# A linear-attention and MLP kernel: k and q loaded as bf16 by casting DMAs and left unscaled, the decay moved to v and to the attention output, stores of 64 rows from SyncE

## The chip, the cores and the metric

The kernel runs on one core of a Trainium2 chip. The metric is the device time in microseconds (us). Before the change it was 261.36 us, the median of two runs (261.17 to 261.54). Profiles come from one execution each; their span is about 2 us shorter than the device time of the same run (259.0 for 260.8). All times below that carry a position ("at 73.4 us") are counted from the start of that span.

## The reference, cut to what matters

```python
# q, k, v: (B=4, H=8, S=768, D=64) float32; lam: (8,), about 0.97 to 0.99
for b in range(S // 64):                       # blocks of 64 positions
    intra = (q_b @ k_b^T) * lam**(i - j) [i >= j] @ v_b
    inter = (q_b * lam**(i + 1)) @ kv_state
    out_b = intra + inter
    kv_state = lam**64 * kv_state + (k_b * lam**(63 - i))^T @ v_b
x = out as (3072 tokens, 512)
h = x @ w_in                                   # 512 -> 2048
g = h + sin(alpha * h)**2 / (alpha + 1e-9)
return g @ w_out                               # 2048 -> 512, float32
```

## The kernel before

The kernel works on blocks of 128 positions and pairs of batches. One *step* is half the heads of one block: transposes of q and k ("T"), scores ("S"), then outputs and the state ("O"). Four steps fill one *chunk* of 512 tokens. A chunk's first matmul is 16 *A groups* (x times w1, four matmuls each), its second 16 *B groups* (g times w2). There are six chunks, 0 to 5; while TensorE works on chunk c, it also does the steps of chunk c+1. The steps 0 to 3 have nothing to hide behind, and steps 4 to 7 are done in the B part of chunk 0.

In the views, PS is a bank of PSUM (the memory that TensorE writes its results to), S_m are the masked scores, xT is the attention output as the first matmul reads it, Zacc the state and Zs its bf16 copy, u and t are steps of the sine and its square, gT is g, and osb is an output tile.

A small planner in Python records every operation with an assumed duration, sorts by planned start time, and emits a fixed order for each engine. Each engine then runs its list strictly in that order. So an assumed duration that is wrong costs nothing in itself, but it can put an instruction that has to wait ahead of one that is ready.

```python
        # decay: q scaled by lam**i, k by lam**-i, per position of the pass; v only cast
        def prep_x(s, x, engs=("POOL", "DVE")):          # x is "q" or "k"
            ...
            rec(eng, lambda e: e.tensor_tensor(dst[c][:, :, :], raw(src, s), L_b, ALU.mult), dur, ...)

        def load(d, x, parts=(0, 1), eng="SP", after=()):  # float32, 64 partitions per DMA
            ...
            nbytes=29375 * nh      # what the planner counts, nh = 8 heads: 235,000

        # attention output, a plain copy on ScalarE
        op = rec("ACT", lambda e: e.copy(xo, xi), 0.6, ...)

        # the store of one output tile
        dst = bass.AP(out.tensor, row0 * DM, [[DM, 2], [2 * DM, 64], [1, DM]])
        rec("ACT", lambda e: e.dma_start(dst, osb[o][:, :]), 0, ...)

        # start: loads of blocks 2 and 3 wait for the third w2 block
        for m0, n in ((0, 2), (2, 2), (4, 4), (8, 4), (12, 4)):
            w1_block(m0, n, after=[v0])
        for j in range(4):
            w2b = w2_block(4 * j, 4, after=[v0])
            if j == 2:
                gate = w2b
        for x in "kqv":
            for d in (2, 3):
                load(d, x, after=[gate])
```

An access pattern is a list of [step, count], slowest first. The store's destination has two as its slowest count: token rows 0, 2, 4, ... come from partitions 0 to 63 and rows 1, 3, 5, ... from partitions 64 to 127. The weights are loaded by GpSimd, which casts them to bf16 on the way.

## Time and profile before

The timeline gives the positions below. "First w1 matmul" is the first A group of chunk 0, and each chunk is counted from its first A group to that of the next chunk.

| stretch | before, us |
|---|---|
| start, to the first w1 matmul | 23.8 |
| chunk 0 | 49.6 |
| chunks 1 to 4 | 138.5 |
| chunk 5, to the end of the last matmul | 30.4 |
| tail, to the end of the span | 16.7 |

The lines below are from the page of the kernel before: busy time of each engine, then the span in 40 equal slices of 6.5 us (busy tenths of TensorE, the TensorE clock that was granted in tenths, and the mean busy share of the 16 DMA engines in tenths), then the DMA queues with their share of 16 engines' span.

```profile
PE 216.0 (83%) x2785; PEld 108.6 (42%) x2785; DVE 136.0 (53%) x190; ACT 129.2 (50%) x203; POOL 119.2 (46%) x137
PE   0448897299589999999999999999999999999400
PEclk9999999658959999999999999999999999999955
DMA  6999999999349996944355110001101011010111
q1 hardware_dynamic: 38016, 18.88, 34.1%
q0 software_dynamic: 4752, 4.19, 10.5%
q10 hardware_dynamic: 3296, 6.30, 6.6%
```

TensorE (PE) is the busiest engine, yet it is full only from the thirteenth slice on. From the second to the tenth slice the row of the DMA engines is full and the row of TensorE is not. At the end TensorE has nothing to do and the DMA row reads 1.

The next view is the table of busy time by stretch, with its header; the first line is the tail, the others ten-microsecond stretches of chunk 0.

```profile
core 0: us, PE busy (x) PEld busy (x) DVE busy (x) ACT busy (x) POOL busy (x), PEclk, DMA share, GB/s
242.40:259.00 16.60, 0.00 (x0) 0.00 (x0) 0.00 (x0) 0.55 (x1) 0.00 (x0) 0.57 0.12 48
...
40.00:50.00 10.00, 3.95 (x19) 1.57 (x16) 3.78 (x6) 0.00 (x0) 4.82 (x5) 0.84 1.06 212
50.00:60.00 10.00, 9.57 (x126) 4.71 (x128) 3.32 (x5) 3.32 (x5) 4.50 (x5) 0.50 1.21 233
60.00:70.00 10.00, 7.89 (x217) 4.58 (x216) 5.97 (x9) 2.34 (x4) 1.83 (x3) 0.98 0.62 156
```

In the tail a share of 0.12 is two engines of sixteen. From 40 to 60 us the share is 1.06 and then 1.21, so the DMA engines are taken to be full (it adds up the times of the packets, and passes 1 where they overlap). TensorE waits from 44 to 50 us, and from 50 to 60 it runs at half its clock.

Finally the chain that ended last, in order of time (start, duration, what). It shows what chunk 0 hung on.

```profile
21.44 17.99 DMA w<-in_moe_w_out_dram
...
56.26 13.87 DMA v<-in_v_dram
70.18 0.62 POOL v L388
70.80 0.36 POOL Zs L549
71.20 0.64 PE PS L428 x8
```

The first line is the wait for w2, behind which the loads of blocks 2 and 3 are held.

### The profile page before, as it was taken

How to read it: one execution, taken by the hardware profiler on the slowest of the kernel's cores; microseconds unless marked ns; L12 is line 12 of the kernel's file. 1: busy time of each engine (PE TensorE's matmuls, PEld its weight loads, DVE VectorE, ACT ScalarE, POOL GpSimd, SP SyncE). 2: the span in 40 equal slices, each digit the busy share in tenths (PEclk: the TensorE clock that was granted, in tenths of full speed). 3: DMA queues.
4: the chain of work that ended last, by engine and by line, in shares of the span. 5: the costliest groups of instructions: out<-in, count | busy, mean ns of one | idle time of the engine just before them, and what ended most of it. 6: DMA issues, size and time to landing. Idle time of an engine off the chain costs nothing.

```text
span 259.0 us, 6365 instructions
## 1 busy us (share of the span) xinstructions
PE 216.0 (83%) x2785; PEld 108.6 (42%) x2785; DVE 136.0 (53%) x190; ACT 129.2 (50%) x203; POOL 119.2 (46%) x137
## 2 busy tenths in 40 slices
PE   0448897299589999999999999999999999999400
PEld 0346343145244445544455544555445544444100
DVE  2582595227317866557754677843687315850000
ACT  5045781040237764377826678446774447642000
POOL 3567764543246784446565464532744107440000
PEclk9999999658959999999999999999999999999955
DMA  6999999999349996944355110001101011010111
GB/s 138 226 166 172 206 206 188 227 228 220 99 154 194 224 193 186 229 134 143 97 157 150 53 51 21 34 12 49 51 17 42 3 43 51 31 40 18 51 51 44
DMA packets 46092, 29.79 MB, mean 115 GB/s; under 512 B 1504, under 2 KB 42992, under 8 KB 46064
## 3 DMA queue, kind: packets, MB, share of 16 engines
q1 hardware_dynamic: 38016, 18.88, 34.1%
q0 software_dynamic: 4752, 4.19, 10.5%
q10 hardware_dynamic: 3296, 6.30, 6.6%
q8 instruction: 22, 0.36, 0.6%
q14 instruction: 6, 0.05, 0.1%
HBM read 27.28 MB, written 6.29 MB: 130 GB/s over the span
## 4 chain that ended last, share of the span: by engine, by line
PE 65%; DMA 15%; SPq 9%; POOL 2%; ACT 1%; issue 1%
PE PS L614 28%; PE PS L577 28%; SPq L298 9%; DMA v<-in_v_dram 8%; DMA w<-in_moe_w_out_dram 7%; PE PS L406 3%; PE PS L438 2%; PE PS L415 2%; POOL w L359 2%; PE PS L428 2%; PE PS L451 1%; POOL w L364 1%; ACT qkT L560 0%; POOL v L388 0%; ACT xT L540 0%
## 5 line engine op out<-in xcount | busy, mean ns | idle before, releaser
L614 PE MATMUL PS<-w,gT 128*128 128x512 bf16 x384 | 93.2, 387 | 0.0
L589 POOL TENSOR_TENSOR u<-t 128x512 bf16<-128x512 bf16 x66 | 67.5, 1041 | 49.8 <-ACT t L581 48.6
L577 PE MATMUL PS<-xT,w 128*128 128x512 bf16 x384 | 88.5, 385 | 2.2 <-ACT xT L540 1.4
L591 DVE SCALAR_TENSOR_TENSOR gT<-u,r_sb,PS 128x512 bf16<-128x512 bf16 x96 | 69.1, 745 | 34.9 <-POOL u L589 34.4
L581 ACT ACTIVATE t<-PS,alpha_sb 128x512 bf16<-128x512 f32 x96 | 63.8, 683 | 23.7 <-PE PS L577 23.0
L577 PEld LDWEIGHTS PS<-xT,w 128*128 128x128 bf16 x384 | 37.7, 99 | 49.3 <-issue 3.8
L614 PEld LDWEIGHTS PS<-w,gT 128*128 128x128 bf16 x384 | 35.9, 99 | 42.6 <-issue 1.8
L523 DVE TENSOR_TENSOR S_m<-PS,mask 128x1024 bf16<-128x1024 f32 x24 | 29.3, 1224 | 29.0 <-PE PS L415 28.8
L540 ACT CAST xT<-PS 128x512 bf16<-128x512 f32 x24 | 14.1, 586 | 39.3 <-PE PS L438 39.2
L406 PE MATMUL PS<-ident,q 64*64 64x64 bf16 x384 | 15.4, 212 | 17.8 <-DVE q L381 17.2
L381 POOL TENSOR_TENSOR k<-k,Lk 128x512 bf16<-128x512 f32 x16 | 17.7, 1107 | 27.4 <-DMA k<-in_k_dram 13.0
L560 ACT COPY qkT<-PS 128x1024 bf16<-128x1024 bf16 x17 | 17.3, 1016 | 16.9 <-PE PS L406 15.8
L406 PEld LDWEIGHTS PS<-ident,q 64*64 64x64 bf16 x384 | 10.4, 119 | 29.0 <-POOL k L381 9.6
L621 ACT COPY osb<-PS 128x512 f32<-128x512 f32 x24 | 14.2, 591 | 16.2 <-PE PS L614 13.6
L428 PE MATMUL PS<-S_m,v 64*64 64x128 bf16 x384 | 14.6, 239 | 3.2 <-POOL Zs L549 3.2
L381 DVE TENSOR_TENSOR q<-q,Lq 128x512 bf16<-128x512 f32 x16 | 11.5, 741 | 10.0 <-DMA q<-in_q_dram 10.0
L438 PE MATMUL PS<-qkT,Zs 64*64 64x128 bf16 x160 | 15.6, 234 | 0.4
L549 POOL CAST Zs<-Zacc 128x256 bf16<-128x256 f32 x16 | 8.0, 498 | 16.5 <-DVE Zacc L547 16.5
L406 PE MATMUL PS<-ident,k 64*64 64x64 bf16 x384 | 14.6, 207 | 0.0
L415 PE MATMUL PS<-qkT 64*64 64x128 bf16 x384 | 13.5, 238 | 1.1 <-ACT qkT L560 0.4
L451 PE MATMUL PS<-v,k 64*64 64x64 bf16 x320 | 11.5, 207 | 1.7 <-issue 1.7
L428 PEld LDWEIGHTS PS<-S_m,v 64*64 64x64 bf16 x384 | 10.5, 118 | 5.8 <-POOL Zs L549 3.7
(40 smaller groups left out, 119.7 us busy)
## 6 DMA issues: line engine op xcount, KB each, us to landing
k<-in_k_dram SPq DMA_DIRECT2D x24, 256.0 KB, 6.5
q<-in_q_dram SPq DMA_DIRECT2D x24, 256.0 KB, 7.1
v<-in_v_dram SPq DMA_DIRECT2D x24, 256.0 KB, 7.1
out_dram<-osb ACTq DMA_DIRECT2D x24, 256.0 KB
w<-in_moe_w_out_dram POOLq DMA_DIRECT2D x4, 512.0 KB, 17.1
w<-in_moe_w_in_dram POOLq DMA_DIRECT2D x3, 512.0 KB, 9.7
w<-in_moe_w_in_dram POOLq DMA_DIRECT2D x2, 256.0 KB, 5.0
lam_bc<-in_lam_dram ACTq DMA_DIRECT2D x1, 4.0 KB, 2.8
```

Of the source, the lines that this page charges most:

```text
L298: op = rec(eng, lambda e, u=u, a=a: e.dma_start(dst[r][half(u), h0:h0 + nh, :], a), 0, writes=[f"{x}32.{r}.{u}.{p}" for p in parts], slot= ...
L381: rec(eng, lambda e: e.tensor_tensor(dst[c][:, :, :], raw(src, s), L_b, ALU.mult), dur, reads=reads, writes=writes)
L406: last = e.transpose(dst, src[half(u), hid(h, tt), :], ident[half(u), half(u)])
L415: return e.matmul(PS[half(u), sb_ + r, (h // 2 * 2 + tj) * 128:(h // 2 * 2 + tj + 1) * 128], qt[half(r), u, 1, h // 2, half(tj)], qt[half( ...
L428: return e.matmul(dst, v2[o % RC][half(u), hid(h, tj), :], S_m[o % RS][half(u), h % 2 ^ u, h // 2, tj, :], start=start, stop=True, skip_gr ...
L438: return e.matmul(dst, Zs[(o - 2) % 3][half(r), u, h // 2, :], qkT[o % RQ][half(r), u, 0, h // 2, :], start=start, stop=True, skip_group_c ...
L523: rec("DVE", lambda e: e.tensor_tensor(S_m[s % RS][:, :, :, :, :].rearrange("p r a t i -> p (r a) (t i)"), PS[:, sb_:sb_ + 2, :].rearrange ...
L577: last = e.matmul(PS[:, i, :], w1[:, kc, 128 * m:128 * (m + 1)], xT[x][:, kc, :], start=(kc == 0), stop=(kc == NKC - 1))
L581: rec("ACT", lambda e: e.activation(t16[tt][:, :], PS[:, i, :], ACTF.Sin, scale=alpha_sb[:, m:m + 1]), 0.7, reads=bk(i) + ["alpha"], write ...
L589: return e.tensor_tensor(u16[tt][:, :], t16[tt][:, :], t16[tt][:, :], ALU.mult)
L591: rec("DVE", lambda e: e.scalar_tensor_tensor(out=gT[g][:, m, :], in0=u16[tt][:, :], scalar=r_sb[:, m:m + 1], in1=PS[:, i, :], op0=ALU.mul ...
L614: last = e.matmul(PS[:, bank, :], gT[g][:, m, 128 * s4:128 * (s4 + 1)], w2[:, m, :], start=(m == 0), stop=(m == NM - 1))
```

## The change

The intent is to take work off the engines in the crowded first 75 us, and to order the loads better. In detail:

- k and q are loaded by GpSimd DMAs that cast to bf16, and are not scaled. The decay is put on v (lam**-j, one multiplication per step) and on the attention output (lam**i, as the output is moved out of PSUM, now on VectorE). A table of lam**i is built at the start.
- Loads of k and q and the weights of chunk 0 are issued one after another on GpSimd, interleaved; squares of chunk 0's A part leave GpSimd for ScalarE and VectorE.
- Each store becomes two of 64 rows, from SyncE.
- The planner counts a float32 load of half a block as 310,000 units instead of 235,000, and a cast load as 171,000. It also keeps the DMA issues of an engine in the order in which they were recorded, and lets a read of a PSUM bank wait for earlier reads of it by other engines.

```diff
-        q2 = ring("q2", RC, [128, 2 * HS, D], BF16)
+        q2 = ring("q2", RL, [128, H, 2 * D], BF16)
...
-                         nbytes=29375 * nh, after=after)
+                op = rec("SP" if x == "v" else "POOL", lambda e, u=u, a=a: e.dma_start(dst[r][half(u), :, :], a), 0,
+                         writes=[f"{x}.{r}.{u}"], slot=f"{x}{r}", nbytes=310000 if x == "v" else 171000, after=after)
...
-        def prep_x(s, x, engs=("POOL", "DVE")):
+        def prep_v(s, engs=("POOL", "DVE")):
+            rec(eng, lambda e: e.tensor_tensor(v2[c][:, :, :], src, L_b, ALU.mult), dur, reads=reads, writes=writes)
...
-                op = rec("ACT", lambda e: e.copy(xo, xi), 0.6, reads=keys_o,
+                rec("DVE", lambda e: e.tensor_tensor(xo, xi, X_b, ALU.mult), 0.72,
...
-                dst = bass.AP(out.tensor, row0 * DM, [[DM, 2], [2 * DM, 64], [1, DM]])
-                rec("ACT", lambda e: e.dma_start(dst, osb[o][:, :]), 0,
+                for t in range(2):
+                    dst = bass.AP(out.tensor, (row0 + t) * DM, [[2 * DM, 64], [1, DM]])
+                    rec("SP", lambda e, t=t, dst=dst: e.dma_start(dst, osb[o][half(t), :]), 0,
...
+        v0 = load(0, "v", after=[k0])
+        load(1, "v", after=[kq])
...
+        ISSUE_A0 = {0: lambda: w2_next(0), 2: lambda: load(2, "k"), 4: lambda: load(2, "q"), 6: lambda: w2_next(1),
+                    8: lambda: load(2, "v", after=[gates[1]]), 9: lambda: load(3, "k"), 12: lambda: load(3, "q"),
+                    14: lambda: w2_next(2)}
+        ISSUE_B0 = {0: lambda: w2_next(3), 1: lambda: load(3, "v", after=[gates[2]]),
+                    9: lambda: load(4, "k"), 10: lambda: load(4, "q"), 11: lambda: load(5, "k"),
+                    12: lambda: load(5, "q")}
```

More of the change, by code (lines that the diff above doesn't have):

```diff
@@ L45, in __init__ @@
         self.dma_free = 0.0
+        self.issued = {e: 0.0 for e in self.ISSUE}
     def deps_of(self, reads, writes):
@@ L89, in add @@
         for b in reads:
+            if b.startswith("b."):
+                op.deps.update(r for r in self.readers.get(b, ()) if r.eng != eng)
+        for b in reads:
             self.readers.setdefault(b, []).append(op)
@@ L102, in add @@
         op.kslot = self.slots[slot]
-        op.start = self.place(eng, t, self.ISSUE[eng])
+        op.start = self.place(eng, max(t, self.issued[eng]), self.ISSUE[eng])
+        self.issued[eng] = op.start
         if nbytes < 10000:
@@ L222, in sem @@
             return es.enter_context(nc.semaphore(name))
-        q32 = ring("q32", RL, [128, H, 2 * D], F32)
-        k32 = ring("k32", RL, [128, H, 2 * D], F32)
         v32 = ring("v32", RL, [128, H, 2 * D], F32)
-        q2 = ring("q2", RC, [128, 2 * HS, D], BF16)
-        k2 = ring("k2", RC, [128, 2 * HS, D], BF16)
+        q2 = ring("q2", RL, [128, H, 2 * D], BF16)
+        k2 = ring("k2", RL, [128, H, 2 * D], BF16)
         v2 = ring("v2", RC, [128, 2 * HS, D], BF16)
@@ L242, in bass_lightning_attn__then__act_snake_kernel @@
         mask2 = ring("mask2", 2, [128, 2, 128], BF16)
-        zeros = sb("zeros", [128, 512], BF16)
         maskf = sb("maskf", [128, 256], F32)
@@ L250, in bass_lightning_attn__then__act_snake_kernel @@
         lnL = sb("lnL", [128, NB, H, 2], F32)
-        Lq = sb("Lq", [128, NB, H, 2], F32)
-        Lk = sb("Lk", [128, NB, H, 2], F32)
+        Lv = sb("Lv", [128, NB, H, 2], F32)
+        X_i = sb("X_i", [128, 2, 64], I32)
+        X_f = sb("X_f", [128, NB, 128], F32)
+        lnlamp = sb("lnlamp", [128, HS], F32)
+        Xt = sb("Xt", [128, HS, NB, 128], F32)
         alpha_r = sb("alpha_r", [NM, 128], F32)
@@ L288, in where, with load @@
             return pair, n, hh
-        def load(d, x, parts=(0, 1), eng="SP", after=()):
+        def load(d, x, after=()):
             pair, n = d // NB, d % NB
             r = d % RL
-            src, dst = {"k": (k, k32), "q": (q, q32), "v": (v, v32)}[x]
-            h0, nh = HS * parts[0], HS * len(parts)
+            src, dst = {"k": (k, k2), "q": (q, q2), "v": (v, v32)}[x]
             for u in range(2):
-                off = (((2 * pair + u) * H + h0) * S + n * BL) * D
-                a = bass.AP(src.tensor, off, [[2 * D, 64], [S * D, nh], [1, 2 * D]])
-                op = rec(eng, lambda e, u=u, a=a: e.dma_start(dst[r][half(u), h0:h0 + nh, :], a), 0,
-                         writes=[f"{x}32.{r}.{u}.{p}" for p in parts], slot=f"{x}{r}{parts[0]}{len(parts)}",
-                         nbytes=29375 * nh, after=after)
+                a = bass.AP(src.tensor, (2 * pair + u) * H * S * D + n * BL * D, [[2 * D, 64], [S * D, H], [1, 2 * D]])
+                op = rec("SP" if x == "v" else "POOL", lambda e, u=u, a=a: e.dma_start(dst[r][half(u), :, :], a), 0,
+                         writes=[f"{x}.{r}.{u}"], slot=f"{x}{r}", nbytes=310000 if x == "v" else 171000, after=after)
             return op
@@ L306, in consts @@
             rec("ACT", lambda e: e.preload_act_table_set("natural_log_exp_and_others"), 1.3, writes=["table"])
-            rec("POOL", lambda e: e.memset(zeros[:, :], 0.0), 0.5, writes=["zeros"])
-            rec("POOL", lambda e: e.iota(E_i[:, :, :, :], [[BL, NB], [0, H], [1, 2]], base=0, channel_multiplier=2), 0.2,
-                writes=["E_i"])
-            for u in range(2):
-                rec("DVE", lambda e, u=u: e.tensor_scalar_add(E_f[half(u), :, :, :], E_i[half(u), :, :, :], -128 * u),
-                    0.2, reads=["E_i"], writes=[f"E_f.{u}"])
-            rec("ACT", lambda e: e.activation(lnlam[:, :], lam_bc[:, :], ACTF.Ln), 0.3,
-                reads=["lam", "table"], writes=["lnlam"])
-            ln_b = bass.AP(lnlam, 0, [[H, 128], [0, NB], [1, H], [0, 2]])
-            rec("DVE", lambda e: e.tensor_tensor(lnL[:, :, :, :], E_f[:, :, :, :], ln_b, ALU.mult), 0.2,
-                reads=["E_f.0", "E_f.1", "lnlam"], writes=["lnL"])
-            rec("ACT", lambda e: e.activation(Lq[:, :, :, :], lnL[:, :, :, :], ACTF.Exp), 0.3,
-                reads=["lnL"], writes=["Lq"])
-            rec("ACT", lambda e: e.activation(Lk[:, :, :, :], lnL[:, :, :, :], ACTF.Exp, scale=-1.0), 0.3,
-                reads=["lnL"], writes=["Lk"])
+            rec("ACT", lambda e: e.dma_start(alpha_r[:, :], moe_alpha.rearrange("(m p) -> m p", p=128)), 0,
+                writes=["alpha_r"], slot="alpha", nbytes=8192)
             rec("DVE", lambda e: e.memset(maskf[:, :], 0.0), 0.2, writes=["maskf"])
@@ L325, in consts @@
                 base=0, channel_multiplier=1), 0.3, reads=["maskf"], writes=["ident"])
+            rec("POOL", lambda e: e.iota(X_i[:, :, :], [[1, 2], [2, 64]], base=0, channel_multiplier=0), 0.2,
+                writes=["X_i"])
+            rec("POOL", lambda e: e.iota(E_i[:, :, :, :], [[BL, NB], [0, H], [1, 2]], base=0, channel_multiplier=2), 0.2,
+                writes=["E_i"])
             for u in range(2):
@@ L331, in consts @@
                     base=-128 * u, channel_multiplier=2), 0.3, reads=["maskf"], writes=[f"mask2.{u}"])
+            rec("POOL", lambda e: e.affine_select(
+                out=identf[:, :], in_=maskf[0:NM, 0:NM], pattern=[[-1, NM]], compare_op=ALU.not_equal, fill=1.0,
+                base=0, channel_multiplier=1), 0.3, reads=["maskf"], writes=["identf"])
+            for n in range(NB):
+                rec("DVE", lambda e, n=n: e.tensor_scalar_add(
+                    X_f[:, n, :], X_i[:, :, :].rearrange("p t i -> p (t i)"), BL * n), 0.15,
+                    reads=["X_i"], writes=[f"X_f.{n}"])
+            for u in range(2):
+                rec("DVE", lambda e, u=u: e.tensor_scalar_add(E_f[half(u), :, :, :], E_i[half(u), :, :, :], -BL * u),
+                    0.2, reads=["E_i"], writes=[f"E_f.{u}"])
+            rec("ACT", lambda e: e.activation(lnlam[:, :], lam_bc[:, :], ACTF.Ln), 0.3,
+                reads=["lam", "table"], writes=["lnlam"])
+            for c in range(2):
+                rec("ACT", lambda e, c=c: e.activation(lnlamp[half(c), :], lam_bc[half(c), c:H:2], ACTF.Ln), 0.3,
+                    reads=["lam", "table"], writes=[f"lnlamp.{c}"])
+            ln_b = bass.AP(lnlam, 0, [[H, 128], [0, NB], [1, H], [0, 2]])
+            rec("DVE", lambda e: e.tensor_tensor(lnL[:, :, :, :], E_f[:, :, :, :], ln_b, ALU.mult), 0.2,
+                reads=["E_f.0", "E_f.1", "lnlam"], writes=["lnL"])
             for u in range(2):
@@ L334, in consts, with decay_table @@
                     reads=[f"mask2.{u}"], writes=[f"mask.{u}"])
-            rec("POOL", lambda e: e.affine_select(
-                out=identf[:, :], in_=maskf[0:NM, 0:NM], pattern=[[-1, NM]], compare_op=ALU.not_equal, fill=1.0,
-                base=0, channel_multiplier=1), 0.3, reads=["maskf"], writes=["identf"])
+            rec("ACT", lambda e: e.activation(Lv[:, :, :, :], lnL[:, :, :, :], ACTF.Exp, scale=-1.0), 0.3,
+                reads=["lnL"], writes=["Lv"])
+        def decay_table(n0, n1):
+            for z in range(HS):
+                rec("ACT", lambda e, z=z: e.activation(
+                    Xt[:, z, n0:n1, :], X_f[:, n0:n1, :], ACTF.Exp, scale=lnlamp[:, z:z + 1]), 0.2 + 0.11 * (n1 - n0),
+                    reads=[f"X_f.{n}" for n in range(n0, n1)] + ["lnlamp.0", "lnlamp.1"],
+                    writes=[f"X.{z}.{n}" for n in range(n0, n1)])
         def sin_table():
             rec("ACT", lambda e: e.activation(junk[:, :], maskf[:, 0:1], ACTF.Sin), 1.5,
-                reads=["maskf", "Lk", "Lq"], writes=["junk"])
+                reads=["maskf", "Lv"] + [f"X.{z}.{n}" for z in range(HS) for n in range(NB)], writes=["junk"])
         def alpha_ops(b):
-            rec("ACT", lambda e: e.dma_start(alpha_r[:, :], moe_alpha.rearrange("(m p) -> m p", p=128)), 0,
-                writes=["alpha_r"], slot="alpha", nbytes=8192)
             rec("PE", lambda e: e.transpose(PS[:, b, 0:NM], alpha_r[:, :], identf[0:NM, 0:NM]), 0.3,
@@ L348, in alpha_ops, with alpha_ops2 @@
             rec("ACT", lambda e: e.copy(alpha_sb[:, :], PS[:, b, 0:NM]), 0.2, reads=bk(b), writes=["alpha"])
+        def alpha_ops2():
             rec("POOL", lambda e: e.tensor_scalar_add(aeps_sb[:, :], alpha_sb[:, :], 1e-9), 0.2,
@@ L365, in w2_block, with part, part_keys, sec @@
                           f"w2_{m0}", n, after)
-        def raw(t, s):
-            hh = s % 2
-            return t[s // 2 % RL][:, HS * hh:HS * hh + HS, :].rearrange("p h (t d) -> p (h t) d", t=2)
-        def raw_keys(x, s):
-            return [f"{x}32.{s // 2 % RL}.{u}.{s % 2}" for u in range(2)]
-        def prep_x(s, x, engs=("POOL", "DVE")):
-            pair, n, hh = where(s)
-            c = s % RC
-            src, dst, L = (q32, q2, Lq) if x == "q" else (k32, k2, Lk)
-            L_b = bass.AP(L, (n * H + HS * hh) * 2, [[NB * H * 2, 128], [1, 2 * HS], [0, D]])
-            reads, writes = raw_keys(x, s) + ["L" + x], [f"{x}2.{c}"]
-            eng, dur = fastest([(e, {"POOL": 1.05, "DVE": 0.75}[e]) for e in engs], reads, writes)
-            rec(eng, lambda e: e.tensor_tensor(dst[c][:, :, :], raw(src, s), L_b, ALU.mult), dur,
-                reads=reads, writes=writes)
-        def prep_v(s):
-            c = s % RC
-            reads, writes = raw_keys("v", s), [f"v2.{c}"]
-            eng, dur = fastest([("ACT", 0.62), ("POOL", 1.05)], reads, writes)
-            rec(eng, lambda e: (e.copy if eng == "ACT" else e.tensor_copy)(v2[c][:, :, :], raw(v32, s)), dur,
-                reads=reads, writes=writes)
+        def prep_v(s, engs=("POOL", "DVE")):
+            pair, n, hh = where(s)
+            c, r = s % RC, s // 2 % RL
+            src = v32[r][:, HS * hh:HS * hh + HS, :].rearrange("p h (t d) -> p (h t) d", t=2)
+            L_b = bass.AP(Lv, (n * H + HS * hh) * 2, [[NB * H * 2, 128], [1, 2 * HS], [0, D]])
+            reads, writes = [f"v.{r}.0", f"v.{r}.1", "Lv"], [f"v2.{c}"]
+            eng, dur = fastest([(e, {"POOL": 1.05, "DVE": 0.65}[e]) for e in engs], reads, writes)
+            rec(eng, lambda e: e.tensor_tensor(v2[c][:, :, :], src, L_b, ALU.mult), dur, reads=reads, writes=writes)
         def hid(h, t):
             return 2 * h + t
-        def sec(t=None, o=None, s=None, tb=None, sb_=S_BK, ob=O_BK, peek=False):
+        def part(t, s, u, h, tt):
+            return t[s // 2 % RL][half(u), HS * (s % 2) + h, D * tt:D * tt + D]
+        def part_keys(x, s):
+            return [f"{x}.{s // 2 % RL}.{u}" for u in range(2)]
+        def sec(t=None, o=None, s=None, tb=None, sb_=S_BK, ob=O_BK, peek=False, t_engs=("DVE", "ACT")):
             po, no, ho = where(o) if o is not None else (0, 0, 0)
@@ L401, in f @@
                 def f(e):
-                    src = (q2, k2)[x][t % RC]
                     for tt in range(2):
@@ L405, in f @@
                         dst = PS[half(h % 2 ^ u), tb[u], :].bitcast(BF16)[:, slot:slot + 64]
-                        last = e.transpose(dst, src[half(u), hid(h, tt), :], ident[half(u), half(u)])
+                        last = e.transpose(dst, part((q2, k2)[x], t, u, h, tt), ident[half(u), half(u)])
                     return last
@@ L450, in f @@
                         started.add((b, c))
-                        last = e.matmul(dst, k2[o % RC][half(u), hid(h, tj), :], v2[o % RC][half(u), hid(h, tj), :],
+                        last = e.matmul(dst, part(k2, o, u, h, tj), v2[o % RC][half(u), hid(h, tj), :],
                                         start=start, stop=True, skip_group_check=True)
@@ L502, in sec @@
                 if has_Z:
-                    reads += [f"k2.{o % RC}"]
+                    reads += part_keys("k", o)
             if t is not None:
-                reads += [f"q2.{t % RC}", f"k2.{t % RC}", "ident"]
+                reads += part_keys("q", t) + part_keys("k", t) + ["ident"]
             if s is not None:
@@ L526, in sec @@
                     reads=keys_s + ["mask.0", "mask.1"], writes=[f"S_m.{s % RS}"])
-            after = ()
             if has_Z:
@@ L532, in sec @@
                 if no == 0:
-                    zeng, dur = fastest([("ACT", 0.37), ("DVE", 0.4)], keys_o, [f"Zs.{o % 3}"])
-                    after = (rec(zeng, lambda e: (e.copy if zeng == "ACT" else e.tensor_copy)(zs, z), dur,
-                                 reads=keys_o, writes=[f"Zs.{o % 3}"]),)
+                    rec("ACT", lambda e: e.copy(zs, z), 0.37, reads=keys_o, writes=[f"Zs.{o % 3}"])
             if o is not None:
@@ L539, in sec @@
                 xi = PS[:, ob:ob + 2, 0:256].rearrange("p u (a i) -> p u a i", a=2)
-                op = rec("ACT", lambda e: e.copy(xo, xi), 0.6, reads=keys_o,
-                         writes=[f"x.{x}.{o % 4}"], after=after)
+                X_b = bass.AP(Xt, (2 * ho * NB + no) * 128, [[HS * NB * 128, 128], [0, 2], [NB * 128, 2], [1, 128]])
+                rec("DVE", lambda e: e.tensor_tensor(xo, xi, X_b, ALU.mult), 0.72,
+                    reads=keys_o + [f"X.{2 * ho + a}.{no}" for a in range(2)],
+                    writes=[f"x.{x}.{o % 4}"])
             if has_Z:
                 if no == 0:
-                    rec("DVE", lambda e: e.tensor_copy(acc[:, :, :], z), 0.4, reads=keys_o,
-                        writes=[f"Zacc.{ho}"], after=(op,))
+                    rec("ACT", lambda e: e.copy(acc[:, :, :], z), 0.4, reads=keys_o, writes=[f"Zacc.{ho}"])
                 else:
                     rec("DVE", lambda e: e.tensor_tensor(acc[:, :, :], z, acc[:, :, :], ALU.add), 0.42,
-                        reads=keys_o + [f"Zacc.{ho}"], writes=[f"Zacc.{ho}"], after=(op,))
+                        reads=keys_o + [f"Zacc.{ho}"], writes=[f"Zacc.{ho}"])
                     rec("POOL", lambda e: e.tensor_copy(zs, acc[:, :, :]), 0.42,
@@ L558, in sec @@
                     to = qkT[j][:, :, :, :, :].rearrange("p u x a i -> p u (x a i)")
-                eng, dur = fastest([("DVE", 0.7), ("ACT", 1.1)], keys_t, [f"qkT.{j}"])
+                eng, dur = fastest([(e, {"DVE": 0.7, "ACT": 1.05}[e]) for e in t_engs], keys_t, [f"qkT.{j}"])
                 rec(eng, lambda e: (e.copy if eng == "ACT" else e.tensor_copy)(to, ti), dur,
@@ L624, in grp_B @@
                 row0 = (2 * pair + u) * S + n * BL
-                dst = bass.AP(out.tensor, row0 * DM, [[DM, 2], [2 * DM, 64], [1, DM]])
-                rec("ACT", lambda e: e.dma_start(dst, osb[o][:, :]), 0,
-                    reads=[f"o.{o}"], slot=f"o{o}", nbytes=128 * 2048)
-            return op
-        def warm(n):
-            def pe(e):
-                for _ in range(n):
-                    last = e.matmul(PS[:, 0, :], ident[:, :], zeros[:, :])
-                return last
-            rec("PE", pe, 0.22 * n, reads=["ident", "zeros"], writes=bk(0))
@@ L637, in bass_lightning_attn__then__act_snake_kernel @@
-        consts()
-        for d in (0, 1):
-            load(d, "k")
-            load(d, "q")
-        v0 = load(0, "v")
-        load(1, "v")
-        sin_table()
-        for m0, n in ((0, 2), (2, 2), (4, 4), (8, 4), (12, 4)):
-            w1_block(m0, n, after=[v0])
-        for j in range(4):
-            w2b = w2_block(4 * j, 4, after=[v0])
-            if j == 2:
-                gate = w2b
-        for x in "kqv":
-            for d in (2, 3):
-                load(d, x, after=[gate])
-        for s in (0, 1):
-            prep_x(s, "k", ("POOL",))
-            prep_x(s, "q")
@@ L656, in bass_lightning_attn__then__act_snake_kernel @@
-        sec(t=0, tb=(0, 1))
-        sec(t=1, tb=(2, 3))
+                for t in range(2):
+                    dst = bass.AP(out.tensor, (row0 + t) * DM, [[2 * DM, 64], [1, DM]])
+                    rec("SP", lambda e, t=t, dst=dst: e.dma_start(dst, osb[o][half(t), :]), 0,
+                        reads=[f"o.{o}"], slot=f"o{o}", nbytes=64 * 2048)
+            return op
+        k0 = load(0, "k")
+        kq = load(0, "q")
+        consts()
+        load(1, "k")
+        load(1, "q")
+        v0 = load(0, "v", after=[k0])
@@ L658, in bass_lightning_attn__then__act_snake_kernel @@
+        load(1, "v", after=[kq])
+        alpha_ops(6)
+        decay_table(0, 2)
+        sec(t=0, tb=(0, 1), t_engs=("DVE",))
+        sec(t=1, tb=(2, 3), t_engs=("ACT",))
         sec(s=0, sb_=4)
-        alpha_ops(6)
-        for s in (2, 3):
-            prep_x(s, "k", ("POOL",))
-            prep_x(s, "q", ("DVE",))
         sec(s=1, sb_=6)
-        sec(t=2, tb=(0, 1))
-        sec(t=3, tb=(2, 3))
-        for s in range(4):
-            prep_v(s)
+        sec(t=2, tb=(0, 1), t_engs=("ACT",))
@@ L668, in bass_lightning_attn__then__act_snake_kernel @@
+        sec(t=3, tb=(2, 3), t_engs=("ACT",))
         sec(s=2, sb_=4)
         sec(s=3, sb_=6)
+        w1_block(0, 2, after=[v0])
+        prep_v(0, ("POOL",))
+        prep_v(1, ("DVE",))
+        w1_block(2, 2, after=[v0])
+        prep_v(2, ("POOL",))
+        prep_v(3, ("DVE",))
+        w1_block(4, 4, after=[v0])
+        w1_block(8, 8, after=[v0])
         sec(o=0, ob=0)
@@ L672, in bass_lightning_attn__then__act_snake_kernel @@
             sec(o=s, ob=2 * s)
-        nl, npr = [4], [4]
+        alpha_ops2()
+        decay_table(2, NB)
+        sin_table()
+        nl, npr = [6], [8]
         def ahead(s):
@@ L678, in ahead @@
                 p = npr[0]
-                prep_x(p, "k")
-                prep_x(p, "q")
                 prep_v(p)
@@ L693, in steady, with w2_next @@
             return sec(t=t, o=o, s=s, tb=(b, b), peek=peek)
+        gates = {}
+        def w2_next(j):
+            gates[j] = w2_block(4 * j, 4)
+        ISSUE_A0 = {0: lambda: w2_next(0), 2: lambda: load(2, "k"), 4: lambda: load(2, "q"), 6: lambda: w2_next(1),
[4 more added lines that the diff above has]
+                    12: lambda: load(5, "q")}
         every, low = range(8), range(4)
@@ L701, in bass_lightning_attn__then__act_snake_kernel @@
         for c in range(NCH):
+            if c == 1:
+                load(4, "v")
+                load(5, "v")
             for m in range(NM):
-                grp_A(c, m, every if m < 12 else range(2, 4) if m == 15 else range(4, 8), (SQ.get(m, "POOL"),))
+                grp_A(c, m, every if m < 12 else range(2, 4) if m == 15 else range(4, 8),
+                      (SQ.get(m, "POOL"),) if c else ("POOL", "ACT", "DVE"))
+                if c == 0 and m in ISSUE_A0:
+                    ISSUE_A0[m]()
                 if c > 0 and m in (3, 7, 11):
                     grp_B(c - 1, 3, m // 4 + 1, low)
-            if c == 0:
-                ahead(7)
             b_seq = [(s4, m4) for m4 in range(4) for s4 in range(2)] + [(2, m4) for m4 in range(4)] + [(3, 0)]
@@ L711, in bass_lightning_attn__then__act_snake_kernel @@
                     steady(B1_SEC[i])
+                if c == 0 and i in ISSUE_B0:
+                    ISSUE_B0[i]()
+                if c == 0 and 4 <= i < 8:
+                    prep_v(i)
                 grp_B(c, s4, m4, low if c else range(2) if s4 < 2 else range(s4 - 2, s4 - 1))
```

## The prediction

> **What bounds the kernel now.** The timeline and the chain of waits split the 259.0 us span into four parts. (1) 0 to 23.8 us: loading, scaling, attention steps 0 to 3; then the first w1 matmul. (2) 23.8 to 73.4: chunk 0. TensorE has only about 14 us (A groups), 11 us (B groups) and 4 attention steps of 1.6 us, 31.5 us in all, so about 18 us are lost. The table of waits names q's scaling (17.2 us, here and at the start); the chain shows why: loads of blocks 2 and 3 sit behind a weight load until 39.4, then DMA v until 70.2. The windows view shows DMA saturated from 10 to 60. (3) 73.4 to 242.4: TensorE 99% busy at full clock, 34.0 us a chunk. (4) 242.4 to 259.0: only the last stores, DMA share 0.12 to 0.13, 46 to 51 GB/s.
>
> **Part 4 is the surest gain.** A share of 1/8 is 2 of 16 DMA engines. [...] 6.6% of 16 engines' span over 3296 packets is 83 ns each; 128 packets on 2 engines are 5.4 us a store. The last four, issued 235.3 to 243.0, queue for 21.5 us, which gives the 259. The new outermost dimension is 64. After the last copy (0.59 us) I expect two SyncE issues (0.6 us each) and roughly 2 us to land: a tail of 4 us for 16.6. Gain about 12.5 us.
>
> **Start.** The scaling of k and q goes (on POOL 1.04 us and more, on VectorE 0.69 each). The first transpose moves from 9.6 to about 6.5. But block 1's k, q still queue, and four S_m of 1.22, two v scalings and four xT products of about 0.7 run in series on VectorE: first w1 matmul at about 22.5. Gain 1 to 2.
>
> **Chunk 0.** POOL issues 48 more loads at about 0.78 us (as the weight loads took), 37 us, for some 35 us of scaling and copying removed: neutral. The bytes read are the same, but k, q of blocks 2, 3 are interleaved with w2. With 2.3 us per f32 load (512 KB at 225 GB/s), 2.6 per w2 block (195 GB/s of bf16) and an estimated 2 us per cast load (between these), the last w2 block and v3 land at about 46. A of chunk 0 takes 16 us, since squares leave POOL for ACT and VectorE. Chunk 1 starts at about 60 for 73.4. Gain about 12 with the start.
>
> **Steady part.** TensorE does the same; VectorE takes xT (24 times 0.7) from ACT and loses scaling. 34 us a chunk stay: 0 to -1.
>
> **Sum.** 261.4 - 12.5 - 12 = about 237 us.
>
> **Right if** the after-profile shows a DMA share well above 0.13 in stores and a tail under 5 us; the first w1 matmul near 22, chunk 1 near 60; chunks still 34 us; a TensorE clock that drops less from 40 to 80.
>
> **Wrong if** a cast load that writes 256 B pieces costs much more than 2 us of saturated DMA [...]: at twice that, chunk 0 gains nothing and the time is near 248. Also wrong if [...] VectorE's longer queue delays xT and stalls TensorE in steady chunks.
>
> Predicted 237 us, 80% range 230 to 247; faster 0.97, within 2% 0.02, slower 0.01.

261.4 less 12.5 for the tail and 12 for the start and chunk 0 is 236.9. What stands behind the 12.5 is the share of 0.12 to 0.13 in the trace of before; that the new shape would raise it had not been shown. For the estimated 0.6 us of an issue and 2 us to land, the medians of the stores in the changed kernel are 0.60 and 2.4 us. In part (3) the mean granted clock was 0.99, since the second stretch at 0.5 lasts until 77.5 us.

## The result, and the profile after

The changed kernel takes 238.96 us, the median of two runs (238.90 to 239.02). The ratio to the kernel before is 0.914, with a 95% interval of 0.910 to 0.918. Ratios here and below are the mean time of one kernel's fast runs over that of the other's of the same rounds, so they are not quite the ratio of the medians that are quoted.

| stretch | before, us | predicted | after, us | difference |
|---|---|---|---|---|
| start | 23.8 | 22.5 | 26.0 | +2.2 |
| chunk 0 | 49.6 | 37.5 | 37.3 | -12.3 |
| chunks 1 to 4 | 138.5 | 0 to 1 less | 139.3 | +0.8 |
| chunk 5 | 30.4 | the same | 30.4 | 0.0 |
| tail | 16.7 | 4 | 4.0 | -12.6 |
| span | 259.0 | | 237.0 | -22.0 |

The same lines of the page for the changed kernel:

```profile
PE 211.7 (89%) x2785; PEld 105.9 (45%) x2785; DVE 139.0 (59%) x201; ACT 122.9 (52%) x189; POOL 122.0 (51%) x154
PE   0416899998899899999999899999999999999993
PEclk9999999999999999999999999999999999999999
DMA  7999999996890892990327890503100204101033
q0 software_dynamic: 29568, 10.49, 38.5%
q1 hardware_dynamic: 16512, 12.59, 21.9%
```

TensorE is at eight tenths or more from the fifth slice to the last but one. Its clock doesn't drop once it is up, but the row hides the beginning: the records of the granted clock start only at 30.1 us here (22.9 in the kernel before), and time without a record counts as full. The nine w1 matmuls that ended before 30.1 us took 626 ns each, the next twenty 379, so chunk 0 began at half rate, which cost about 2 us of it (an estimate: ten matmuls that follow each other at 427 instead of 216 ns). The casting loads now sit on q0; the stores have joined v's loads on q1, and q10, which was ScalarE's, is out of use but for the two small loads at the start. The stretches and the chain:

```profile
233.00:237.00 4.00, 0.00 (x0) 0.00 (x0) 0.00 (x0) 0.58 (x1) 0.00 (x0) 1.00 0.28 66
...
40.00:50.00 10.00, 9.86 (x103) 4.77 (x101) 6.19 (x11) 5.11 (x9) 1.54 (x1) 1.00 1.33 210
50.00:60.00 10.00, 9.08 (x262) 5.28 (x262) 7.04 (x9) 2.94 (x4) 2.69 (x4) 1.00 0.91 142
60.00:70.00 10.00, 9.07 (x100) 4.29 (x87) 6.10 (x11) 4.78 (x8) 6.71 (x10) 1.00 1.07 183
```

```profile
8.09 7.86 DMA q<-in_q_dram
16.09 0.69 PE PS L412 x32
16.80 1.02 ACT qkT L564
18.64 2.35 DVE S_m L529 x2
25.12 0.69 DVE xT L544
...
32.68 10.42 DMA w<-in_moe_w_out_dram
43.76 8.41 DMA v<-in_v_dram
52.19 0.69 DVE v L391
```

The tail is 4.0 us, with a mean DMA share of 0.28, which includes the copy and the issues ahead of the transfers; from 235 to 236 us the share is 0.87. Chunk 0 still shows two long DMA waits in the chain, but TensorE has other work under them: 9.86 of 10 us against 3.95 before. The start is the one stretch that became longer. Its chain is a wait for q of block 1 until 16.1 us and then a row of VectorE work.

### The profile page after: what moved, and what is told of

The parts are those of the page before. It is cut to its first block, busy times and chain, and to the rows that moved or that the text cites. A ratio compares the mean times of both kernels' runs of the same rounds, so it can differ in the third digit from the quotient of the medians.

```text
span 237.0 us, 6359 instructions
## 1 busy us (share of the span) xinstructions
PE 211.7 (89%) x2785; PEld 105.9 (45%) x2785; DVE 139.0 (59%) x201; ACT 122.9 (52%) x189; POOL 122.0 (51%) x154
## 3 DMA queue, kind: packets, MB, share of 16 engines
q0 software_dynamic: 29568, 10.49, 38.5%
## 4 chain that ended last, share of the span: by engine, by line
PE 71%; DMA 11%; DVE 6%; POOL 6%; issue 2%; ACT 2%; SPq 0%; POOLq 0%; ACTq 0%
PE PS L618 30%; PE PS L581 28%; DMA w<-in_moe_w_out_dram 4%; PE PS L412 4%; DMA v<-in_v_dram 4%; DMA q<-in_q_dram 3%; DVE S_m L529 3%; PE PS L444 3%; PE PS L434 3%; PE PS L421 3%; POOL k L301 2%; POOL q L301 2%; DVE xT L544 1%; PE PS L457 1%; ACT qkT L564 1%
## 5 line engine op out<-in xcount | busy, mean ns | idle before, releaser
L618 PE MATMUL PS<-w,gT 128*128 128x512 bf16 x384 | 90.6, 380 | 0.0
L595 DVE SCALAR_TENSOR_TENSOR gT<-u,r_sb,PS 128x512 bf16<-128x512 bf16 x96 | 69.8, 746 | 35.2 <-POOL u L593 32.0
L593 POOL TENSOR_TENSOR u<-t 128x512 bf16<-128x512 bf16 x55 | 56.8, 1051 | 35.7 <-ACT t L585 35.5
L581 PEld LDWEIGHTS PS<-xT,w 128*128 128x128 bf16 x384 | 37.3, 99 | 49.9 <-issue 3.9
L564 ACT COPY qkT<-PS 128x1024 bf16<-128x1024 bf16 x21 | 21.2, 1013 | 38.7 <-PE PS L421 32.4
L391 POOL TENSOR_TENSOR v<-v,Lv 128x512 bf16<-128x512 f32 x16 | 17.9, 1118 | 25.6 <-DMA v<-in_v_dram 14.3
L301 POOL DMA_DIRECT2D k<-in_k_dram x24 | 17.3, 742 | 7.9 <-PE PS L444 4.0
L553 POOL CAST Zs<-Zacc 128x256 bf16<-128x256 f32 x16 | 6.5, 403 | 27.3 <-DVE Zacc L551 27.3
L544 DVE TENSOR_TENSOR xT<-PS,Xt 128x512 bf16<-128x512 f32 x24 | 16.4, 682 | 2.4 <-PE PS L444 2.3
L301 POOL DMA_DIRECT2D q<-in_q_dram x24 | 17.0, 735 | 0.0
L434 PE MATMUL PS<-S_m,v 64*64 64x128 bf16 x384 | 14.3, 235 | 1.5 <-DVE v L391 1.5
L592 ACT ACTIVATE u<-t 128x512 bf16<-128x512 bf16 x24 | 15.1, 629 | 1.0
```

The source lines that it names most:

```text
L301: op = rec("SP" if x == "v" else "POOL", lambda e, u=u, a=a: e.dma_start(dst[r][half(u), :, :], a), 0, writes=[f"{x}.{r}.{u}"], slot=f"{x} ...
L434: return e.matmul(dst, v2[o % RC][half(u), hid(h, tj), :], S_m[o % RS][half(u), h % 2 ^ u, h // 2, tj, :], start=start, stop=True, skip_gr ...
L564: rec(eng, lambda e: (e.copy if eng == "ACT" else e.tensor_copy)(to, ti), dur, reads=keys_t, writes=[f"qkT.{j}"])
L581: last = e.matmul(PS[:, i, :], w1[:, kc, 128 * m:128 * (m + 1)], xT[x][:, kc, :], start=(kc == 0), stop=(kc == NKC - 1))
L593: return e.tensor_tensor(u16[tt][:, :], t16[tt][:, :], t16[tt][:, :], ALU.mult)
L595: rec("DVE", lambda e: e.scalar_tensor_tensor(out=gT[g][:, m, :], in0=u16[tt][:, :], scalar=r_sb[:, m:m + 1], in1=PS[:, i, :], op0=ALU.mul ...
```

## The experiments

All twelve are listed by stretch here, as the timeline of each profile gives it; times are medians. Names that begin with b_ are edits of the kernel before, those with a_ of the changed kernel.

| kernel | time | start | chunk 0 | chunks 1 to 4 | tail |
|---|---|---|---|---|---|
| before | 261.4 | 23.8 | 49.6 | 138.5 | 16.7 |
| changed | 239.0 | 26.0 | 37.3 | 139.3 | 4.0 |
| b_st64_act | 249.0 | 23.9 | 47.6 | 139.8 | 4.1 |
| b_st64_sp | 248.5 | 23.5 | 50.0 | 140.6 | 4.0 |
| a_st128_sp | 280.7 | 25.8 | 37.7 | 165.5 | 16.7 |
| b_gate0 | 260.2 | 23.4 | 49.7 | 139.1 | 16.7 |
| b_model | 259.8 | 24.2 | 47.8 | 139.3 | 16.6 |
| b_order_model | 255.8 | 23.0 | 45.6 | 137.6 | 16.7 |
| b_warm | 273.0 | 23.7 | 60.7 | 140.3 | 16.7 |
| b_warm0 | 261.5 | 24.8 | 49.9 | 138.4 | 16.7 |
| b_order_warm | 254.7 | 24.0 | 44.3 | 137.5 | 16.7 |
| a_oldorder | 240.8 | 26.9 | 38.8 | 138.6 | 4.1 |
| a_vlater | 243.0 | 25.9 | 41.1 | 138.2 | 4.0 |
| a_v3first | 239.1 | 27.0 | 36.9 | 138.4 | 4.0 |

Chunk 5 took 30.4 or 30.5 us in all of them. The time of a_oldorder is that of its one fast run, that of b_order_warm the median of its five fast runs of six. The start moves by about a microsecond between kernels that share it.

### The stores, their shape and their engine

b_st64_act puts the two stores of 64 rows into the kernel before and leaves them on ScalarE.

```diff
-                dst = bass.AP(out.tensor, row0 * DM, [[DM, 2], [2 * DM, 64], [1, DM]])
-                rec("ACT", lambda e: e.dma_start(dst, osb[o][:, :]), 0, ...
+                for t in range(2):
+                    dst = bass.AP(out.tensor, (row0 + t) * DM, [[2 * DM, 64], [1, DM]])
+                    rec("ACT", lambda e, t=t, dst=dst: e.dma_start(dst, osb[o][half(t), :]), 0, ...
```

> The kernel before with only the stores cut into two of 64 rows, still issued from ScalarE. Theory A (the prediction: the two-engine store costs only in the tail): tail from 16.6 to about 4 us, chunk 0 unchanged, chunk 1 still starts near 73.4 us, time about 249 us. Theory B (the two engines that carry stores also hold back the loads of chunk 0, because the trace of before shows the DMA share falling to about 0.3 from 59 to 75 us while a load is still being waited for): the tail gain and in addition the stall of 66 to 71 us gone, chunk 1 starts near 67, time 242 to 244 us. Theory C (it is the issuing engine, not the shape): about 261 us.

b_st64_sp is the same edit with "SP" in place of "ACT".

> The kernel before with the new stores in full: two of 64 rows, issued from SyncE. If only the shape matters, within 1 us of the same stores from ScalarE. If SyncE's in-order waits for output tiles delay loads that are issued behind them, slower than those by some us. If the issuing engine were what mattered (theory C), this one alone gains 12 us or more.

The first took 248.98 us (ratio 0.952, 0.949 to 0.955), the second 248.47 (0.949, 0.943 to 0.954). Theory A holds: the shape is worth 12.6 us in the tail, on either engine, and theory C is out. Theory B is wrong for the time: with ScalarE chunk 0 and chunk 1 are 2 us shorter each, and later chunks give most of it back. These edits also change the order that the planner emits for the other engines, from about 66 us on in b_st64_act, so differences of 1 or 2 us outside the tail can't be put down to the stores. The tail of b_st64_act in the table by stretch:

```profile
241.70:245.80 4.10, 0.01 (x1) 0.00 (x0) 0.00 (x0) 0.58 (x1) 0.00 (x0) 0.98 0.28 64
```

a_st128_sp is the converse, the old shape in the changed kernel, from SyncE.

```diff
-                for t in range(2):
-                    dst = bass.AP(out.tensor, (row0 + t) * DM, [[2 * DM, 64], [1, DM]])
-                    rec("SP", lambda e, t=t, dst=dst: e.dma_start(dst, osb[o][half(t), :]), 0, ...
+                dst = bass.AP(out.tensor, row0 * DM, [[DM, 2], [2 * DM, 64], [1, DM]])
+                rec("SP", lambda e: e.dma_start(dst, osb[o][:, :]), 0, ...
```

> The changed kernel with the old shape of store (one of 128 rows, outermost dimension 2), from SyncE. Theory A: only the tail comes back, 239 + 12.5 = 251.5 us, and chunk 1 still starts near 63 us. Theory B: loads of v on the same queue are held too, chunk 1 starts later, 253 to 260 us. Theory C (issuing engine): 239 us.

It took 280.67 us (ratio 1.073 to the kernel before), far outside what either theory said. The tail came back as expected (16.7 us), but chunks 1 to 4 grew by 26 us as well. SyncE's own part of the timeline shows why; the lines are those of the changed kernel first,

```profile
49.66 11.72 SPq L631 DMA_DIRECT2D out_dram<-osb  x6
61.43 2.74 SPq L301 DMA_DIRECT2D v<-in_v_dram  x4
```

and of a_st128_sp, with a stretch of its table that follows and two lines of its chain:

```profile
50.09 10.86 SPq L630 DMA_DIRECT2D out_dram<-osb  x3
60.99 9.20 SPq L301 DMA_DIRECT2D v<-in_v_dram  x4
...
73.00:83.00 10.00, 5.21 (x18) 1.69 (x16) 4.75 (x7) 3.47 (x6) 6.98 (x7) 0.83 0.06 13
...
84.64 10.33 DMA v<-in_v_dram
...
107.25 14.66 DMA v<-in_v_dram
```

SyncE reaches the four v loads at the same time in both (61.0 and 61.4 us), so it isn't its wait for output tiles that holds them up. Issuing them takes 9.20 us behind three stores of 128 rows on the same queue and 2.74 us behind six of 64 rows, and the loads then land late: in the chain they are waited for 10 to 15 us at a time. While TensorE is half idle from 73 to 83 us, only 0.06 of the DMA engines' time is used, one engine of sixteen. So in the kernel before the old shape cost little outside the tail, and there the stores had a queue of their own (ScalarE's). In the change the new shape and the new engine are not independent: with the old shape on SyncE, the changed kernel is slower than the kernel before. That the shared queue is the reason is read from these lines. The planner's order on VectorE and GpSimd changes too, but first at about 88 us, after the first late load; and the old shape from ScalarE in the changed kernel, which would settle it, was not run.

### Order of loads and order of instructions in chunk 0

b_gate0 changes one number in the kernel before.

```diff
-            if j == 2:
+            if j == 0:
                 gate = w2b
```

> The kernel before with one number changed: the loads of blocks 2 and 3 are released by the landing of w2's first block and not of its third. Theory A (order of loads is what chunk 0 gained from): the idle of TensorE from 44 to 50 us shrinks, chunk 1 starts 5 to 8 us earlier, 253 to 256 us. Theory B: the first idle moves, but the wait for block 4's v remains, so 258 to 261 us.

It took 260.22 us (ratio 0.996, 0.994 to 0.999); the expectation of theory A failed. The first transposes of block 2 came at 50.7 us instead of 50.2: loads released 4 us earlier share the DMA engines with w2 (in the kernel before their share is 1.20 from 30 to 40 us), and the q that the transposes need is fifth and sixth in line. This was a poor test of order, since only the release moved.

b_model changes only the planner's number.

```diff
-                         nbytes=29375 * nh, after=after)
+                         nbytes=38750 * nh, after=after)
```

> The kernel before with one number in the planner that places instructions: a load of half a block is counted as 310,000 units in place of 235,000, as in the change. No instruction is added or removed; only the order on GpSimd, VectorE and ScalarE changes (the state copy Zs of blocks 2 and 3 comes ahead of the cast of block 4's v on GpSimd). Theory O (the idle of TensorE from 66 to 71 us is an in-order wait: GpSimd stands at a cast whose data have not landed while Zs waits behind it): chunk 1 starts about 4 to 5 us earlier, near 69 us, time about 257 us. Theory D (chunk 0 is limited by the DMA engines' throughput alone): chunk 1 stays near 73, time 261 us.

It took 259.83 us (0.995, 0.990 to 1.000). The in-order wait at 66 to 71 us is gone, but chunk 0 became only 1.9 us shorter, less than half of what theory O said. In its profile the half-clock stretch was longer (17.1 us instead of 13.7), from 48.5 us on, and the steps in it followed each other at 3.1 to 3.5 us, as in the kernel before.

b_order_model adds the stepwise release of the loads.

```diff
         for m0, n in ((0, 2), (2, 2), (4, 4), (8, 4), (12, 4)):
-            w1_block(m0, n, after=[v0])
-        ...
-        for x in "kqv":
-            for d in (2, 3):
-                load(d, x, after=[gate])
+            w1b = w1_block(m0, n, after=[v0])
+        w2b = [w2_block(4 * j, 4, after=[v0]) for j in range(4)]
+        for x, d, gate in (("k", 2, w1b), ("q", 2, w1b), ("k", 3, w2b[0]), ("q", 3, w2b[0]), ("v", 2, w2b[1]),
+                           ("v", 3, w2b[2])):
+            load(d, x, after=[gate])
```

> The same, and the loads of blocks 2 and 3 are released step by step, k and q of block 2 as soon as w1 has landed, the others one by one as w2 lands, all still float32 from SyncE with the scaling. Theory A (the order of issue is what chunk 0 gained from): no idle of TensorE ahead of the first transposes of chunk 0, chunk 1 starts at 62 to 65 us, time 250 to 253 us. Theory D (throughput: without the smaller and cheaper cast loads and without the removed scaling no order helps): no more than 2 us better than with the planner's number alone, 255 us or more.

It took 255.77 us (0.979, 0.974 to 0.985): 4 us of the 12.3 in chunk 0, so neither theory as stated. The first transposes came 24.0 us after the first w1 matmul (26.4 before, 21.1 in the changed kernel).

a_oldorder goes the other way, with the order of before in the changed kernel.

```diff
-        ISSUE_A0 = {0: lambda: w2_next(0), 2: lambda: load(2, "k"), ...
+        def late():
+            for x in "kqv":
+                for d in (2, 3):
+                    load(d, x, after=[gates[2]])
+        ISSUE_A0 = {0: lambda: w2_next(0), 1: lambda: w2_next(1), 2: lambda: w2_next(2), 3: lambda: w2_next(3), 4: late}
```

> The changed kernel with the order of issue of before in chunk 0: all four w2 loads first, then k, q and v of blocks 2 and 3, released by the third w2 block. Theory A (order): the transposes of block 2 wait, chunk 1 starts at 67 us or later, time 243 us or more. Theory D (throughput; the bytes are the same and the cast loads are cheap): w2 lands at about 37 us, k and q of both blocks about 7 us later, chunk 1 still near 63 us, time 238 to 241 us.

Its only fast run took 240.8 us, so there is no interval. In that run chunk 0 is 1.5 us longer than in the changed kernel; theory A, which said 243 us or more, does not hold for it. The other three took 245.0 to 247.3 us at a mean granted clock of 0.970 to 0.972 instead of 0.996 and were slow; they are not used. With one run of four left, what the old order costs in the changed kernel stays unsure. By these runs order accounts for 1.5 us here and, with the planner's number, for 4 us there.

### The halved clock

The granted clock is 0.5 in two stretches of chunk 0 of the kernel before (46.8 to 60.4 and 70.7 to 77.5 us); in the changed kernel the half-rate beginning of chunk 0 is the only one. The clock is the number before the last two in these one-microsecond stretches:

```profile
46.00:47.00 1.00, 0.00 (x0) 0.00 (x0) 0.00 (x0) 0.00 (x0) 0.10 (x1) 0.89 1.22 224
59.00:60.00 1.00, 1.00 (x5) 0.16 (x5) 1.00 (x2) 0.00 (x0) 0.65 (x1) 0.50 1.22 257
76.00:77.00 1.00, 1.00 (x4) 0.43 (x3) 0.00 (x0) 0.05 (x1) 0.87 (x1) 0.50 0.40 124
```

The two stretches are 13.7 and 6.8 us long and begin 2.8 and 2.6 us after TensorE's last matmul. Is the clock a cause of lost time of its own? b_warm fills the idle stretches with needless matmuls.

```diff
+                    if i in (5, 12):
+                        warm({5: 26, 12: 18}[i], {5: 7, 12: 4}[i])     # matmuls of zeros, free PSUM bank
```

> The kernel before with 26 and 18 needless matmuls put into the two idle stretches of TensorE in chunk 0 (ahead of the first transposes at 44 us and ahead of the last step at 67 us), into PSUM banks that are free then. Theory K (the halved TensorE clock after idle stretches costs time of its own): the granted clock stays at 1.0 from 44 to 75 us, chunk 1 starts 0 to 3 us earlier and its first 16 matmuls take 3.5 us instead of 5.6, time 257 to 259 us. Rival: the clock is only a companion of the waits, time within 0.7 us of 261.4, or longer if the added matmuls delay the transposes.

It took 273.01 us and says nothing of the clock: the planner counted the added matmuls, and its order on the other engines changed, with the waits that follow from that. b_warm0 (here against b_warm) counts them as zero, and the order on VectorE, ScalarE and GpSimd is then that of before.

```diff
-            rec("PE", pe, 0.22 * n, reads=["ident", "zeros"], writes=bk(b))
+            rec("PE", pe, 0.0, reads=["ident", "zeros"], writes=bk(b))
-                        warm({5: 26, 12: 18}[i], {5: 7, 12: 4}[i])
+                        warm({5: 27, 12: 14}[i], {5: 7, 12: 4}[i])
```

> A better form of the inconclusive test with needless matmuls: the same kernel before with 27 and 14 of them in the two idle stretches of chunk 0, but the planner counts them as zero, so the order on every other engine is exactly that of before. Theory K (half the clock after idle stretches costs time of its own): no half-clock stretch between 44 and 75 us, the three B steps of 3.1 to 3.5 us take 1.9 us, and chunk 1 starts about 3 to 4 us earlier; its first 16 matmuls take 3.5 us and not 5.6; time 255 to 259 us. Rival (the clock only accompanies the waits, data come no sooner): time within 1 us of 261.

It took 261.51 us (1.002, 0.997 to 1.006). Its row of granted clock and two lines of TensorE in its timeline (the bracket is the idle time just before and what ended it):

```profile
PEclk9999999999999999999999999999999999999955
...
67.70 3.19 PE L633 MATMUL PS<-zeros,ident 128*128 128x512 bf16 x13
72.73 0.42 PE L428 MATMUL PS<-S_m,v 64*64 64x128 bf16 x16 [1.85 <-POOL Zs L549]
```

The clock stays up, the B steps follow each other at 1.9 to 2.5 us (one at 3.8), and nothing is gained: TensorE arrives earlier at the wait for Zs, behind GpSimd's cast of block 4's v, and waits longer there (3.2 us of fillers and then 1.85 us idle, against 3.2 us idle before). Theory K falls for the kernel as it stood. The halved clock accompanied the waits there.

b_order_warm asks the same of the kernel in which order and planner are mended, with 20 fillers ahead of the first transposes.

> The kernel before with the planner's number and the stepwise order of loads (255.8 us as it stood), and 20 needless matmuls, counted as zero by the planner, in the 4.3 us idle stretch ahead of the first transposes of chunk 0. Every other order is that of the run without them. Theory P (chunk 0 of before has two limits side by side, the late loads with the in-order wait and the halved clock, so that removing one alone gives little): with loads and order mended the clock is the limit that remains, no half-clock stretch, chunk 1 starts at 64 to 65.5 us and not 68.6, time 251 to 253 us. Rival (the clock costs nothing here either, as in the run that filled the idle stretches of the kernel before as it stands): within 1 us of 255.8. What then still separates it from the changed kernel's 239 plus its 12.5 us of tail is the share of the cast loads and the scaling.

```diff
+                    if i == 5:
+                        warm(20, 7)
```

Its five fast runs have a median of 254.7 us (0.976, 0.971 to 0.980; a sixth, of 257.7, was slow) beside 255.77 for the same kernel without fillers. The part from the first transposes to chunk 1 shrank from 21.6 to 18.2 us, but the transposes themselves came at 50.1 instead of 47.0: in this execution the B part began 3.1 us later (chunk 0 began 0.9 later, and its first 12 w1 matmuls took 630 ns each, at half rate, which none did in b_order_model's), and the fillers ran past the arrival of q, whose scaling ended at 47.1. So here up to 3.4 us may be the clock's, the time does not show it, and the test leaves it open.

### The start, and v of block 3

a_vlater delays the first v loads of the changed kernel; the order of instructions is untouched.

```diff
-        load(1, "k")
+        k1 = load(1, "k")
         load(1, "q")
-        v0 = load(0, "v", after=[k0])
-        load(1, "v", after=[kq])
+        v0 = load(0, "v", after=[kq])
+        load(1, "v", after=[k1])
```

> The changed kernel, the order of instructions on every engine untouched; only the first loads of v wait longer (v of block 0 for q of block 0 instead of k, v of block 1 for k of block 1 instead of q of block 0). Theory S (the start lost 2 us because v's loads take the DMA engines from k and q of block 1): transposes of block 1 at 13 to 14 us and not 16.1, first w1 matmul at 23 to 24.5 us, time 1 to 2.5 us below 239. Rival (the start is limited by the sum of the six loads, or by VectorE's queue): first w1 matmul still within 0.7 us of 26, time 239 us.

It took 243.01 us (0.932, 0.926 to 0.938). Theory S failed: v was issued from 7.6 us on instead of 5.3, yet block 1's transposes came at 15.6 instead of 16.1 us, and the first w1 matmul at 25.9. The weights wait for v, so the first of them was issued 4.3 us later, and chunk 0 grew by 3.8 us. A half-clock stretch of 3.4 us, from 56.5 us on, fell into it as well.

a_v3first holds back the loads of blocks 4 and 5 in the changed kernel.

```diff
-                    9: lambda: load(4, "k"), ...
+                    9: lambda: load(4, "k", after=[gates["v3"]]), ...
```

> The changed kernel, with k and q of blocks 4 and 5 issued only when v of block 3 has landed. If the rest of chunk 0 waits for v of block 3 (the chain of the changed kernel has 8.4 us of it), that v lands at about 47 us and not 52, chunk 1 starts 1 to 3 us earlier, 236 to 238 us; if TensorE's own work is the limit there (its B steps already follow each other at 1.9 us), no gain, 238.5 to 239.5 us.

It took 239.08 us (0.916, 0.912 to 0.921), as the changed kernel did. The v of block 3 came about 1.3 us earlier (GpSimd began to scale it at 50.9 us, where VectorE had begun at 52.2), although chunk 0 began 1.1 us later; that is less than the expected 47. The wait left the chain and chunk 0 was 0.4 us shorter. The chain had named 8.4 us of waiting for this v, but TensorE had other work meanwhile; a long piece in the chain is not a gain by itself. No run beat the changed kernel.

## Why the prediction was right or wrong

The prediction was right: 237 us predicted, 238.96 measured, inside 230 to 247. Point by point:

- **Tail.** Predicted 4 us for 16.6, measured 4.0 for 16.7. The cause stood in the profile: a share of 0.12, and a backlog of four stores that adds up to within about 2 us of the end. That it goes with the shape of the store was not shown there; two experiments whose edit is the stores alone show it (12.6 us of tail, whichever engine issues).
- **Start.** Predicted a gain of 1 to 2 us, measured a loss of 2.2. The step that failed is "First w1 matmul at about 22.5". The first transpose did move, from 9.6 to 7.7 us. But block 1's transposes came at 16.1 us instead of 14.3, and the chain from there to the first w1 matmul took 9.9 us, about as before (9.5), with two S_m, two v scalings and the xT products on VectorE. The later landing of block 1's q was not foreseen. The traces show the larger part of it: the last of these loads was issued at 8.1 us, by GpSimd, which built constants from 4.2 to 6.0 us between the loads of blocks 0 and 1; in the kernel before SyncE issued it at 6.3. It then took 7.9 us to land, where no q load of the start took more than 7.2 before. No run moved the constants, so this is read and not tested; delaying v's issue by 2.3 us moved the landing by only 0.5.
- **Chunk 0.** Predicted to start chunk 1 at 60 for 73.4, measured 63.3, 2.2 of the difference being the later start; the length was predicted as 37.5 and measured as 37.3. The A part took 15.9 us, predicted 16, but some 2 us of that are the half-rate beginning, which the prediction did not have, so this agreement is in part luck. The last w2 block landed at about 46 us as predicted, v of block 3 at 52 and not 46, which a_v3first shows to have cost little. The reason was only partly right. The prediction named the interleaved order of loads. Order, with the planner's number, gave 4.0 us in the kernel before, and undoing it took back 1.5 in the one fast run. The in-order wait on GpSimd at 70 us was seen in the chain but not named as a matter of instruction order; taking it away alone gave 1.9. What no run of the kernel before with float32 loads and scaling reached is the remaining 7 us (44.3 of b_order_warm against 37.3). Those came together with cast loads, unscaled k and q, squares that left GpSimd and the planner's two new rules; they are got by subtraction, were not isolated from each other, and up to 3 of them are the fillers that ran too long in that run.
- **Cost of a cast load.** This was named as the main danger. The page's queue lines give it: 4752 weight packets of before took 10.5% of 16 times 259 us, 92 ns each. Taking those from q0 of the changed kernel (38.5% of 16 times 237 us over 29568 packets) leaves 41 ns for a cast packet, against 37 ns for a float32 packet of before (34.1%, 38016). Sorted by size, the packets of the traces give 41.7 (256 B) and 37.9 ns (512 B). The trace has no sign of the doubled cost. But at 1024 packets on 16 engines the load of a block is 2.7 us, not the 2 that the prediction estimated, against 2.4 in float32: by this measure the cast saves no time of the DMA engines, and the 7 us above are not such a saving.
- **Steady part.** Predicted 0 to 1 us less, measured 0.8 more. Chunk 1 was 0.7 shorter, chunks 2 to 4 together 1.5 longer. VectorE's new work did not hold up TensorE by much: TensorE waited 1.7 us in all for xT. GpSimd's total came out neutral, as predicted (119.2 us busy before, 122.0 after), but by another sum: 34.3 us of load issues for 35.1 of scaling and casts, as predicted, and 17.9 us of v's scaling, which the prediction left out, for the 10.7 of squares that left.
- **What the prediction did not see** is that store shape and store engine hang together. It priced the stores at 12.5 us, which is right for the change as it was made, but with the engine changed and the shape kept the kernel is 42 us slower.

## What to carry to other kernels

Read the DMA share in a tail as a count of engines: 0.12 is two of sixteen. Then try another shape of the transfer: here the share was 0.12 over a tail of 16.7 us with a destination whose slowest count is two, and 0.28 over one of 4 us with two stores whose slowest count is 64. Before moving transfers to another queue, ask what else is on that queue: by the reading above, slow stores held up the loads behind them for 26 us here. In a statically ordered program test a named wait by removing it: removing the long wait for block 3's v, or the halved clock, changed no time as the kernels stood, and removing the in-order wait on GpSimd by another order made chunk 0 only 1.9 us shorter.
